# Signs taken from the scaled words, and sixty matmuls on a zero tile in the attention stage

## The chip, the cores and the metric

The kernel runs on one core of a Trainium2 chip. The metric is the device time of one execution in microseconds; the time of a kernel is the median of its runs. The core has five engines that run side by side and wait for each other by semaphores: PE (TensorE, the matmuls; PEld is its loading of weights), DVE (VectorE), ACT (ScalarE), POOL (GpSimd) and SP, which here only issues DMAs. Each engine works through its own instructions in the order in which they were put down.

## The reference

Three stages follow each other; all inputs are float32 in meaning, but the weights arrive as float64 words.

```python
# B, H, S, D = 2, 8, 768, 64;  n_sink = 4, window = 128
scores = scale * q @ k.T
keep = (key < n_sink) | ((0 <= query - key) & (query - key < window))
a = softmax(where(keep, scores, -1e9))
x = (a @ v) as 1536 tokens x 512
# phase 0: 512 -> 2048 -> 512
h = maximum(x @ w_in, 0);  x = (h * h) @ w_out
# phase 1: 512 -> 2048 -> 512
h = x @ w_in2
P = a0 + a1*h + a2*h**2 + a3*h**3
Q = 1 + abs(b0)*abs(h) + abs(b1)*h**2
out = (P / (Q + 1e-6)) @ w_out2
```

## The kernel before, in words

**Attention** goes by 24 steps (batch, block of 256 queries, pair of heads). A step's work is a generator in four pieces (lines 304 to 391): scores of two query blocks by matmul (`s`, L329, or L331 and L332 for batch 1), mask and row maximum on DVE (L340, L341), exponentials on ACT (L348), division (`rs` on DVE, L352 on POOL); then the transposes `pt` and `sx` on PE (L357, L360) and their copies; then the product with the values `xo` (L382 to L386), which ACT and DVE split into a high part `xh` (L389) and a low part `xl` (L390). `att_pieces` (L491) interleaves three steps: the two score pieces of step t, one piece of step t-1, one of step t-2.

**The two dense phases** use float32 in two parts: each product is three matmuls, high by high, low by high and high by low. A unit is one chunk of 128 hidden columns for one group of 512 tokens (256 in the first sub-chunk of phase 0): `gemm1` (L394) makes `h` by 12 matmuls, ACT and DVE apply the function (`sq`, L128 and L130, in phase 0), ACT rounds it to `gh` (L407), POOL takes the rest `gl` (L409); `gemm2` (L415) adds 12 matmuls into four accumulators. The first units run between the last attention steps.

**Weights** come in chunks of 1024 columns (`load_chunk`, L292), each in two halves of 512 columns. One half passes through `narrowed` (L53): a DMA brings the float64 words into `wr` (three buffers); its high words `hi` lie at every second position. ACT scales them by 2^-112 into `wt` (L63, two buffers) and writes their sign into the upper half of a word of a `sign` tile (L65, two tiles in turn). DVE ORs the shifted low words with the sign (L66, result back in `wr`) and merges them into `wt` (L67). Then ACT rounds `wt` to `wh` (L299) and POOL writes the remainder `wl` (L300), after which `wt` is free; `wr` is free after L67. There are seven chunk slots in the attention stage and four more after it; a chunk's slot is loaded anew when the last group of tokens has used it, so loading comes in four bursts after the start.

**The order.** A scheduler of the framework puts the instructions of each engine into an order by a timeline that it estimates; the code's order and the dependences between tiles are what it starts from. Whatever it puts first on an engine must finish before the next one there starts.

Of the kernel before, what the change touches and what calls it, by code (L numbers as in the profile page):

```python
# [8 lines left out]
F32 = mybir.dt.float32  # L9
F32R = mybir.dt.float32r  # L10
F16 = mybir.dt.float16
# [9 lines left out]
P = 128  # L21
# [12 lines left out]
SC = (6, 5, 5)  # L34
WSLOTS = 7
MORE = 4
RATE = 0.5
LN2_64 = 64.0 * math.log(2.0)


def f32(ap):
    return ap.bitcast(F32)
# [10 lines left out]
def narrowed(nc, pool, src, n, signs):  # L53

    raw = pool.tile([P, 512, 2], U32, tag="wr", name=f"wr{n}", bufs=3)
    nc.sync.dma_start(raw.rearrange("p c w -> p (c w)"), src.bitcast(U32))
    lo, hi = raw[:, :, 0], raw[:, :, 1]
    t = pool.tile([P, 512], U32, tag="wt", name=f"wt{n}")
    s = signs[0]
    signs.append(signs.pop(0))  # L60


    nc.scalar.mul(f32(t), f32(hi), 2.0**-112)  # L63

    nc.scalar.mul(s.bitcast(F16).rearrange("p (c w) -> p c w", w=2)[:, :, 1], f32(hi), 2.0**-112)  # L65
    nc.vector.scalar_tensor_tensor(out=lo, in0=lo, scalar=29, in1=s, op0=ALU.logical_shift_right, op1=ALU.bitwise_or)  # L66
    nc.vector.scalar_tensor_tensor(out=t, in0=t, scalar=3, in1=lo, op0=ALU.logical_shift_left, op1=ALU.bitwise_or)  # L67
    return f32(t)
# [3 lines left out]
def body(ctx, tc, qk0, qk1, vb, vs, nw, wp, ab, out):  # L72
# [32 lines left out]
    with ExitStack() as fast:  # L105

        banded(fast, tc, const, qk0, qk1, vb, vs, rawf[:, 0:1], rawf[:, 2:3], wp, abt, scalars, out)
# [68 lines left out]
def banded(ctx, tc, const, qk0, qk1, vb, vs, ns_f, win_f, wp, ab, scalars, out):  # L176
    nc = tc.nc
# [4 lines left out]
    gpool = ctx.enter_context(tc.tile_pool(name="gpool", bufs=2))  # L182
# [4 lines left out]
    ps_a2 = att_ctx.enter_context(tc.tile_pool(name="ps_a2", bufs=2, space=PSUM))  # L187
# [15 lines left out]
    def load_pair(bb, j, hp):  # L203
        n = f"{bb}_{j}_{hp}"
        w = 256 + (K0 if j == 0 else K1)
        src = qk0[bb, hp] if j == 0 else qk1[bb, j - 1, hp]

        if bb == 0:
            r = at.tile([P, 256 + K1], F32, tag="qkr", name=f"qkr{n}", bufs=3)
            nc.sync.dma_start(r[:, :w], src)  # L210
            qk = r, None
        else:
            qk = [], []
            for hd in range(2):

                r = at.tile([P, 256 + K1], F32, tag="qkr", name=f"qkr{n}{hd}", bufs=3)
                for i in range(2):
                    nc.sync.dma_start(r[i * D : i * D + D, :w], src[hd * D : hd * D + D])
                t = at.tile([P, 256 + K1], F32R, tag="qk", name=f"qk{n}{hd}", bufs=3)
                kl = at.tile([P, K1], F32R, tag="kl", name=f"kl{n}{hd}", bufs=3)  # L220
                nc.scalar.copy(t[:, :w], r[:, :w])

                nc.vector.tensor_tensor(out=t[64:128, :256], in0=r[64:128, :256], in1=f32(t[64:128, :256]), op=ALU.subtract)
                nc.gpsimd.tensor_tensor(out=kl[:, : w - 256], in0=r[:, 256:w], in1=f32(t[:, 256:w]), op=ALU.subtract)
                qk[0].append(t)
                qk[1].append(kl)
        nb = 2 if j == 0 else 3
        v = at.tile([P, 3, P], F32, tag="v", name=f"v{n}")
        nc.sync.dma_start(v[:, :nb, :], vb[bb, 2 * j + 2 - nb : 2 * j + 2, :, hp * P : (hp + 1) * P].rearrange("i p d -> p i d"))
        if bb not in vst:  # L230

            r = wraw.tile([P, 512, 2], U32, tag="wr", name=f"vsr{bb}", bufs=3)
            r = f32(r.rearrange("p c w -> p (c w)"))[:, : HP * P].rearrange("p (h c) -> p h c", h=HP)
            nc.sync.dma_start(r, vs[bb])
            vh = at.tile([P, HP, P], F32R, tag="vsh", name=f"vsh{bb}", bufs=2)
            vl = at.tile([P, HP, P], F32R, tag="vsl", name=f"vsl{bb}", bufs=2)
            nc.scalar.copy(vh, r)
            nc.gpsimd.tensor_tensor(out=vl, in0=r, in1=f32(vh), op=ALU.subtract)
            vst[bb] = vh, vl
        loaded[bb, j, hp] = *qk, v  # L240

    load_pair(0, 0, 0)


    ident = ac.tile([P, P], F32, name="ident")
# [46 lines left out]
    def load_chunk(L, pool=wpool):  # L292
        home[L] = pool
        h = pool.tile([P, 1024], F32R, tag="wh", name=f"wh{L}")
        lo = pool.tile([P, 1024], F32R, tag="wl", name=f"wl{L}")
        for i in range(2):
            c = slice(i * 512, (i + 1) * 512)
            t = narrowed(nc, wraw, wp[L][:, c], f"{L}_{i}", signs)
            nc.scalar.copy(h[:, c], t)  # L299
            nc.gpsimd.tensor_tensor(out=lo[:, c], in0=t, in1=f32(h[:, c]), op=ALU.subtract)  # L300
        wh[L], wl[L] = h, lo
# [173 lines left out]
    start = [(g, c0, 256) for g in range(3) for c0 in (0, 256)]  # L475
# [15 lines left out]
    def att_pieces():  # L491
        live = {}
        for t in range(len(todo) + 2):
            for s_ in (t, t - 1, t - 2):
                if s_ < 0 or s_ >= len(todo):
                    continue
                if s_ == t:
                    live[s_] = attention(*todo[s_])
                    if fetch:
                        load_pair(*fetch.pop(0))  # L500
                    for _ in range(2):
                        next(live[s_])
                        yield
                else:
                    next(live[s_])
                    yield
            if t >= 2:
                done[t - 2] = True

    att = att_pieces()  # L510

    def att_until(step):
# [21 lines left out]
    for i2 in range(N):  # L534
        look = 2 if i2 < n0 else 3
        work = []
        while i1 < N and i1 <= i2 + look:
# [3 lines left out]
            if i1 == n0:  # L541
                att_ctx.close()
                tb = ctx.enter_context(tc.tile_pool(name="tb", bufs=3))

                more = ctx.enter_context(tc.tile_pool(name="more", bufs=MORE))
                for _ in range(MORE):
                    load_chunk(nxt, more)
# [9 lines left out]
        for w_ in work:  # L557
            for _ in w_:
                if i2 < n0:

                    owed += RATE
                    while owed >= 1:
# [10 lines left out]
def dense(tc, qk0, qk1, vb, ns_f, win_f, wp, ab, out):  # L573
# [75 lines left out]
    with xT_ctx, ExitStack() as ctx:  # L649
        wk = ctx.enter_context(tc.tile_pool(name="d_f", bufs=2))  # L650
        ps_a = ctx.enter_context(tc.tile_pool(name="d_pa", bufs=4, space=PSUM))
        ps_h = ctx.enter_context(tc.tile_pool(name="d_ph", bufs=2, space=PSUM))
        for ph in range(2):
            X = yT if ph else xT
            for g in range(NT // 512):
                cols = slice(g * 512, (g + 1) * 512)
                acc = [ps_a.tile([P, 512], F32, tag="acc", name="d_acc") for _ in range(4)]
                for f in range(NF):
                    wi = narrowed(nc, wk, wp[ph * NF + f][:, 0:512], f"d{ph}{g}{f}i", signs)
                    wo = narrowed(nc, wk, wp[ph * NF + f][:, 512:1024], f"d{ph}{g}{f}o", signs)  # L660
                    h = ps_h.tile([P, 512], F32, tag="h", name="d_h")
                    for k in range(4):
                        nc.tensor.matmul(h, lhsT=wi[:, k * P : (k + 1) * P], rhs=X[:, k, cols], start=k == 0, stop=k == 3)
                    y = rational(nc, wk, h, ab, con) if ph else squared_relu(nc, wk, h)
                    for m in range(4):
                        blk = slice(m * P, (m + 1) * P)
                        l, r = (y[:, blk], wo) if ph else (wo[:, blk], y)
                        nc.tensor.matmul(acc[m], lhsT=l, rhs=r, start=f == 0, stop=f == NF - 1)
                for m in range(4):
                    if ph == 0:  # L670
                        nc.vector.tensor_copy(yT[:, m, cols], acc[m])
                    else:
                        o = wk.tile([P, 512], F32, tag="o", name="d_out")
                        nc.scalar.mul(o, acc[m], -1.0)
                        t0 = g * 512 + m * P
                        nc.sync.dma_start(out[t0 : t0 + P, :], o)
# [58 lines left out]
```

## Time and profile before

| what | value |
|---|---|
| median of 3 runs | 687.01 us (686.88 to 688.39) |
| the profiled execution, its own time | 685.88 us |
| its span (first to last instruction) | 684.2 us |
| busy: PE, PEld | 648.0 us (95%), 528.2 us (77%) |
| busy: DVE, ACT, POOL | 467.9, 460.1, 401.5 us |
| bytes read from HBM | 50.27 MB |

The profile is one execution. Busy time is a share of the whole span, and the stages differ: attention runs from 0 to about 206 us with the first dense units in it, the first instructions of phase 1 stand at about 410 us. A matmul counts as busy for its whole duration whatever the clock of TensorE is, so a slow matmul looks busier than a fast one.

### The profile page before, as it was taken

The numbers are of one execution on the slowest core, as the hardware profiler recorded it, in microseconds if no ns is written. First come the engines' busy times: TensorE is split into PE (matmuls) and PEld (weight loads), VectorE is DVE, ScalarE is ACT, GpSimd is POOL, SyncE is SP. The second block draws the span as 40 slices with busy tenths as digits, with TensorE's granted clock in tenths as the row PEclk, the third lists the DMA queues.
The fourth block names the chain that finished last, engine by engine and source line by source line (L and its number), as shares of the span: only waits on it lengthen the run. The fifth ranks groups of instructions, "written<-read, shape, count | busy, mean of one in ns | idle before, by whom it ended". The sixth has DMA issues, their size and how long they took to land.

```text
span 684.2 us, 10131 instructions
## 1 busy us (share of the span) xinstructions
PE 648.0 (95%) x3376; PEld 528.2 (77%) x3376; DVE 467.9 (68%) x969; ACT 460.1 (67%) x938; POOL 401.5 (59%) x367
## 2 busy tenths in 40 slices
PE   4799999999999997999999998899998999999995
PEld 2456779999999875888778886688887888888884
DVE  7878855879842897427631279976699777577674
ACT  6767755777654876427542489886899866766761
POOL 4757855788753776327454579654577644544441
PEclk9999999999999999899999999999999999999998
DMA  7546632354200645204500033200030000001011
GB/s 249 186 134 184 204 90 69 103 135 131 67 25 1 210 160 182 65 1 137 171 0 1 0 124 103 82 1 1 1 123 32 0 1 1 0 1 61 3 61 68
DMA packets 25725, 54.16 MB, mean 79 GB/s; under 512 B 2880, under 2 KB 11072, under 8 KB 25664
## 3 DMA queue, kind: packets, MB, share of 16 engines
q1 hardware_dynamic: 25664, 53.43, 24.5%
q8 instruction: 29, 0.48, 0.3%
q14 instruction: 32, 0.26, 0.1%
HBM read 50.27 MB, written 3.15 MB: 78 GB/s over the span
## 4 chain that ended last, share of the span: by engine, by line
PE 63%; DVE 16%; ACT 8%; DMA 7%; issue 3%; POOL 2%; DVEq 0%; POOLq 0%; ACTq 0%
PE h L400 27%; PE acc L441 14%; PE acc L439 13%; DMA wr<-in_wp 6%; DVE wt L67 5%; DVE wr L66 4%; PE xo L382 3%; ACT sign L65 2%; PE pt L357 1%; PE s L329 1%; ACT wh L299 1%; ACT wt L63 1%; PE xo L385 1%; PE s L332 1%; POOL wl L300 1%
## 5 line engine op out<-in xcount | busy, mean ns | idle before, releaser
L409 POOL TENSOR_TENSOR gl<-sq,gh 128x256 fp32r<-128x256 f32 (+1 forms) x66 | 72.0, 1093 | 80.3 <-ACT gh L407 45.8
L164 POOL TENSOR_TENSOR z<-z,u 128x512 f32<-128x512 f32 x48 | 63.6, 1326 | 84.8 <-ACT z L163 81.5
L300 POOL TENSOR_TENSOR wl<-wt,wh 128x512 fp32r<-128x512 f32 x64 | 91.4, 1439 | 19.9 <-ACT wh L299 19.9
L66 DVE SCALAR_TENSOR_TENSOR wr<-wr,sign 128x512 uint32<-128x512 uint32 x64 | 64.2, 1003 | 19.6 <-ACT sign L65 19.5
L409 POOL TENSOR_TENSOR gl<-z,gh 128x512 fp32r<-128x512 f32 x47 | 62.1, 1322 | 24.8 <-ACT gh L407 21.2
L67 DVE SCALAR_TENSOR_TENSOR wt<-wt,wr 128x512 uint32<-128x512 uint32 x64 | 68.4, 1069 | 10.9 <-ACT wt L63 10.3
L130 DVE TENSOR_TENSOR sq<-sq,h 128x256 f32<-128x256 f32 (+1 forms) x66 | 35.5, 538 | 58.9 <-ACT sq L128 58.1
L439 PE MATMUL acc<-gh,wh 128*128 128x256 f32 (+1 forms) x264 | 66.2, 339 | 5.6 <-ACT sq L128 4.1
L65 ACT ACTIVATE sign<-wr 128x512 f16<-128x512 f32 x64 | 50.6, 790 | 24.6 <-DMA wr<-in_wp 24.4
L439 PE MATMUL acc<-gl,wh 128*128 128x256 f32 (+1 forms) x264 | 64.9, 336 | 0.5 <-POOL gl L409 0.5
L439 PE MATMUL acc<-gh,wl 128*128 128x256 f32 (+1 forms) x264 | 64.7, 334 | 0.0
L170 DVE SCALAR_TENSOR_TENSOR z<-z,con,h 128x512 f32<-128x512 f32 x48 | 35.8, 745 | 41.6 <-ACT h L169 40.1
L400 PE MATMUL h<-xh,wh 128*128 128x256 f32 (+1 forms) x264 | 61.6, 347 | 0.5 <-DVE sq L130 0.5
L128 ACT ACTIVATE sq<-h 128x256 f32<-128x256 f32 (+1 forms) x66 | 31.5, 477 | 45.3 <-PE h L400 34.5
L441 PE MATMUL acc<-wh,gh 128*128 128x512 f32 x192 | 60.2, 393 | 1.2 <-ACT gh L407 1.2
L441 PE MATMUL acc<-wl,gh 128*128 128x512 f32 x192 | 59.6, 390 | 0.0
L400 PE MATMUL h<-x2h,wh 128*128 128x512 f32 x192 | 53.9, 398 | 4.6 <-DVE z L172 4.6
L400 PE MATMUL h<-xl,wh 128*128 128x256 f32 (+1 forms) x264 | 58.2, 337 | 0.0
L400 PE MATMUL h<-xh,wl 128*128 128x256 f32 (+1 forms) x264 | 58.2, 338 | 0.0
L441 PE MATMUL acc<-wh,gl 128*128 128x512 f32 x192 | 57.6, 389 | 0.0
L439 PEld LDWEIGHTS acc<-gh,wh 128*128 128x128 f32 x264 | 44.5, 192 | 13.4 <-ACT wh L299 4.8
L352 POOL TENSOR_TENSOR e<-e,rs 128x320 f32<-128x320 f32 x48 | 37.2, 778 | 28.0 <-DVE rs L350 20.4
(104 smaller groups left out, 1591.9 us busy)
## 6 DMA issues: line engine op xcount, KB each, us to landing
wr<-in_wp SPq DMA_DIRECT2D x64, 512.0 KB, 3.7
qkr<-in_qk SPq DMA_DIRECT2D x32, 176.0 KB, 3.1
v<-in_vb SPq DMA_DIRECT2D x16, 192.0 KB, 2.7
out<-accsb SPq DMA_DIRECT2D x12, 256.0 KB, 2.1
qkr<-in_qk SPq DMA_DIRECT2D x8, 352.0 KB, 3.5
qkr<-in_qk SPq DMA_DIRECT2D x16, 136.0 KB, 2.8
qkr<-in_qk SPq DMA_DIRECT2D x4, 272.0 KB, 5.0
v<-in_vb SPq DMA_DIRECT2D x8, 128.0 KB, 3.6
```

The costliest lines, as they stand in the source:

```text
L65: nc.scalar.mul(s.bitcast(F16).rearrange("p (c w) -> p c w", w=2)[:, :, 1], f32(hi), 2.0**-112)
L66: nc.vector.scalar_tensor_tensor(out=lo, in0=lo, scalar=29, in1=s, op0=ALU.logical_shift_right, op1=ALU.bitwise_or)
L67: nc.vector.scalar_tensor_tensor(out=t, in0=t, scalar=3, in1=lo, op0=ALU.logical_shift_left, op1=ALU.bitwise_or)
L130: nc.vector.tensor_tensor(out=r, in0=r, in1=h, op=ALU.mult)
L164: nc.gpsimd.tensor_tensor(out=z, in0=z, in1=u, op=ALU.mult)
L170: nc.vector.scalar_tensor_tensor(out=z, in0=z, scalar=con[:, 2:3], in1=h, op0=ALU.add, op1=ALU.mult)
L300: nc.gpsimd.tensor_tensor(out=lo[:, c], in0=t, in1=f32(h[:, c]), op=ALU.subtract)
L352: nc.gpsimd.tensor_tensor(out=eq, in0=eq, in1=rs[:, c].unsqueeze(2).to_broadcast([P, 2, W]), op=ALU.mult)
L400: nc.tensor.matmul(h[:, :n], lhsT=w_[:, k * P : (k + 1) * P], rhs=x_[:, k, c0 : c0 + n], start=p_ + k == 0, stop=p_ + k == 5)
L409: eng.tensor_tensor(out=gl[:, :n], in0=y, in1=f32(gh[:, :n]), op=ALU.subtract)
L439: nc.tensor.matmul(acc[m][:, :n], lhsT=w_[:, 512 + m * P : 512 + (m + 1) * P], rhs=g_[:, :n], start=st, stop=sp, skip_group_check=True)
L441: nc.tensor.matmul(acc[m], lhsT=g_[:, m * P : (m + 1) * P], rhs=w_[:, 512:1024], start=st, stop=sp)
```

## The change

Two edits. In `narrowed` the signs are written from `wt`, the scaled copy that L63 has just made, in place of the strided high words in `wr`. In `banded`, a tile `idle` of 128x512 zeros is made on POOL right after the first attention load; it takes one of the two `gh` buffers, and an accumulator tile of the first units serves as output. `keep_busy` issues ten matmuls of 128x512 on it, once ahead of the attention and once after the score pieces of each of the steps 0 to 4: sixty in all. Only the first of each ten is held at its place in the program's order. Nobody reads what they write.

```diff
@@ constants
+IDLE = 10
@@ narrowed
     nc.scalar.mul(f32(t), f32(hi), 2.0**-112)
 
-    nc.scalar.mul(s.bitcast(F16).rearrange("p (c w) -> p c w", w=2)[:, :, 1], f32(hi), 2.0**-112)
+    nc.scalar.mul(s.bitcast(F16).rearrange("p (c w) -> p c w", w=2)[:, :, 1], f32(t), 1.0)
@@ banded, after load_pair(0, 0, 0)
+    idle = gpool.tile([P, 512], F32R, tag="gh", name="idle")
+    nc.gpsimd.memset(f32(idle), 0.0)
@@ att_pieces
                     for _ in range(2):
                         next(live[s_])
                         yield
+                    if t <= 4:
+                        keep_busy()
@@ ahead of att = att_pieces()
+    idle_ps = ps_a2.tile([P, 512], F32, tag="acc", name="idle_ps")
+
+    def keep_busy():
+        for i in range(IDLE):
+            ins = nc.tensor.matmul(idle_ps, lhsT=idle[:, 0:P], rhs=idle, start=True, stop=True)
+            if i == 0:
+                tc.keep_in_program_order(ins)
+
+    keep_busy()
     att = att_pieces()
```

Because the scheduler makes the order, both edits move instructions on every engine. Three places matter below. The line numbers of the changed kernel are higher by 1 to 4 here: L64 is the old L63 (`wt`), L66 the old L65 (`sign`), L67 and L68 the old L66 and L67, L129 the old L128, L303 the old L299, L411 the old L407.

First, PE at the start of attention; names end in batch block, pair of heads and tile number. Before:

```order
L329 MATMUL s_0_0_00_167<-qkr_0_0_103 128x160
L329 MATMUL s_0_0_01_169<-qkr_0_0_103 128x160
L329 MATMUL s_0_0_10_178<-qkr_0_0_103 128x288
L329 MATMUL s_0_0_11_180<-qkr_0_0_103 128x288
L329 MATMUL s_0_1_00_259<-qkr_0_1_159 128x160
```

Now:

```order
L521 MATMUL idle_ps<-idle 128x512 x10
L333 MATMUL s_0_0_00_180<-qkr_0_0_103 128x160
L333 MATMUL s_0_0_01_182<-qkr_0_0_103 128x160
L333 MATMUL s_0_0_10_191<-qkr_0_0_103 128x288
L333 MATMUL s_0_0_11_193<-qkr_0_0_103 128x288
L521 MATMUL idle_ps<-idle 128x512 x10
L333 MATMUL s_0_1_00_282<-qkr_0_1_172 128x160
```

Ten matmuls stand ahead of the first scores, and ten between each two steps; the later tens stand just ahead of the transposes of the step before.

Second, DVE after the masks are made. Before:

```order
L341 ISA e_0_0_166,nm_0_0_163<-s_0_0_01_169,add_115 128x160
L341 ISA nm_0_0_163 128x1
L340 COPY_PREDICATED s_0_0_10_178<-own_u,s_0_0_10_178 128x128
L341 ISA e_0_0_166,nm_0_0_163<-s_0_0_10_178,add_116 128x160
L341 ISA nm_0_0_163 128x1
L340 COPY_PREDICATED s_0_0_11_180<-own_u,s_0_0_11_180 128x128
L349 TENSOR_SCALAR rs_0_0_165<-sm_0_0_164 128x2
```

Now:

```order
L345 ISA e_0_0_179,nm_0_0_176<-s_0_0_01_182,add_117 128x160
L345 ISA nm_0_0_176 128x1
L67 SCALAR_TENSOR_TENSOR wr_0_206<-wr_0_206,sign_93 128x512
L344 COPY_PREDICATED s_0_0_10_191<-own_u,s_0_0_10_191 128x128
L344 COPY_PREDICATED s_0_0_11_193<-own_u,s_0_0_11_193 128x128
L353 TENSOR_SCALAR rs_0_0_178<-sm_0_0_177 128x2
L68 SCALAR_TENSOR_TENSOR wt_0_208<-wt_0_208,wr_0_206 128x512
```

The OR of the first half of weights, which came after the maxima of steps 0 and 1 began, now stands ahead of the second half of step 0.

Third, ACT in the first burst of weights after attention, at the last chunk of phase 0 (chunk 15; `wr_0` and `wr_1` are its halves). Before:

```order
L65 ACTIVATE sign_94<-wr_1_3321 128x512
L63 ACTIVATE wt_0_3314<-wr_0_3312 128x512
L65 ACTIVATE sign_93<-wr_0_3332 128x512
L63 ACTIVATE wt_1_3323<-wr_1_3321 128x512
L299 CAST wh_3310<-wt_0_3314 128x512
L128 ACTIVATE sq<-h 128x512
```

Now:

```order
L64 ACTIVATE wt_0_3377<-wr_0_3375 128x512
L66 ACTIVATE sign_93<-wt_0_3377 128x512
L411 CAST gh<-sq 128x512
L64 ACTIVATE wt_1_3386<-wr_1_3384 128x512
L66 ACTIVATE sign_94<-wt_1_3386 128x512
L303 CAST wh_3373<-wt_0_3377 128x512
L129 ACTIVATE sq<-h 128x512
```

Before, a sign of a later half stood ahead of the scaling of an earlier one. Now each sign follows its own scaling, here and in all 64 halves.

## Rows read from the trace of the kernel before

**Rows 1.** The page, the span in 40 slices: busy tenths of PE, granted clock.

```profile
PE   4799999999999997999999998899998999999995
PEclk9999999999999999899999999999999999999998
```

**Rows 2.** Busy time by stretch; columns PE, PEld, DVE, ACT, POOL, clock, DMA.

```profile
0.00:52.00 52.00, 37.88 (x129) 22.02 (x130) 40.21 (x141) 36.18 (x99) 30.55 (x38) 1.00 0.58 191
52.00:85.00 33.00, 30.26 (x192) 22.80 (x190) 30.09 (x92) 25.41 (x72) 25.62 (x27) 0.95 0.63 195
```

**Rows 3.** Timeline of PE: start, us, what.

```profile
45.79 1.33 PE L329 MATMUL s<-qkr 64*128 64x288 f32 x2 [0.53 <-DVE xl L390]
...
52.90 0.72 PE L329 MATMUL s<-qkr 64*128 64x288 f32 x2 [0.28 <-DVE nm L341]
```

**Rows 4.** The chain of waits in order of time, about 25 to 55 us.

```profile
29.68 0.66 PE sx L360 x2
...
50.79 1.31 PE s L329 x4
```

**Rows 5.** The chain of waits in order of time, 255 to 285 us.

```profile
275.00 1.28 PE acc L439 x3
...
280.10 2.73 PE acc L439 x12
```

**Rows 6.** Timelines of DVE, ACT and POOL at the start.

```profile
8.53 0.28 DVE L340 COPY_PREDICATED s<-own_u,s 128x128 f32<-128x128 uint32 x1
11.08 0.69 DVE L66 SCALAR_TENSOR_TENSOR wr<-wr,sign 128x512 uint32<-128x512 uint32 x1 [0.68 <-ACT sign L65]
9.73 0.65 ACT L63 ACTIVATE wt<-wr 128x512 f32<-128x512 f32 x1
10.29 0.76 ACT L65 ACTIVATE sign<-wr 128x512 f16<-128x512 f32 x1
0.80 0.99 POOL L49 MEMSET sign<- 128x512 uint32 x2 [0.29 <-POOLq L725]
```

**Rows 7.** Groups by line, whole run: busy, mean ns, idle before.

```profile
L65 ACT ACTIVATE sign<-wr 128x512 f16<-128x512 f32 x64 | 50.6, 790 | 24.6 <-DMA wr<-in_wp 24.4
L63 ACT ACTIVATE wt<-wr 128x512 f32<-128x512 f32 x64 | 42.3, 663 | 4.4 <-POOL wl L300 4.2
L299 ACT CAST wh<-wt 128x512 fp32r<-128x512 f32 x64 | 38.9, 617 | 11.5 <-DVE wt L67 11.4
L66 DVE SCALAR_TENSOR_TENSOR wr<-wr,sign 128x512 uint32<-128x512 uint32 x64 | 64.2, 1003 | 19.6 <-ACT sign L65 19.5
L67 DVE SCALAR_TENSOR_TENSOR wt<-wt,wr 128x512 uint32<-128x512 uint32 x64 | 68.4, 1069 | 10.9 <-ACT wt L63 10.3
L300 POOL TENSOR_TENSOR wl<-wt,wh 128x512 fp32r<-128x512 f32 x64 | 91.4, 1439 | 19.9 <-ACT wh L299 19.9
```

**Rows 8.** Busy time by stretch, as rows 2, in bursts of weight loading.

```profile
238.00:255.00 17.00, 16.97 (x73) 13.33 (x72) 15.93 (x16) 13.90 (x26) 13.03 (x9) 1.00 0.51 177
255.00:272.00 17.00, 12.93 (x55) 9.87 (x53) 12.07 (x15) 11.72 (x21) 10.80 (x9) 0.96 0.49 163
272.00:289.00 17.00, 16.47 (x62) 13.29 (x63) 9.23 (x14) 8.32 (x15) 6.53 (x6) 0.84 0.29 96
510.00:527.00 17.00, 15.23 (x67) 12.11 (x66) 16.93 (x20) 17.00 (x31) 12.22 (x10) 1.00 0.10 32
```

**Rows 9.** Timelines of ACT and PE in the first burst.

```profile
261.74 0.78 ACT L65 ACTIVATE sign<-wr 128x512 f16<-128x512 f32 x1 [1.64 <-DMA wr<-in_wp]
265.31 0.60 ACT L128 ACTIVATE sq<-h 128x512 f32<-128x512 f32 x1
272.53 0.76 PE L439 MATMUL acc<-gh,wh 128*128 128x512 f32 x1 [4.05 <-ACT sq L128]
```

**Rows 10.** Timelines of DVE and ACT: the last half kept ready, and the next scaling.

```profile
86.39 0.69 DVE L66 SCALAR_TENSOR_TENSOR wr<-wr,sign 128x512 uint32<-128x512 uint32 x1
...
220.14 0.67 ACT L63 ACTIVATE wt<-wr 128x512 f32<-128x512 f32 x1
```

## The prediction, made before the changed kernel ran

> **What bounds the kernel now.** I read the busy tenths first. PE is at nine tenths or more in nearly every slice after the fifth [rows 1], so whatever moves the time does so by bringing PE to that state earlier, or by filling the few holes behind it. Two kinds of hole are left. One is the start: up to 52 us PE counts as busy for 37.9 us and idle for 14.1 [rows 2], and its matmuls are slow ones. A pair of score matmuls takes 1.33 us at 45.79 and 0.72 us at 52.90 [rows 3]; the ratio 0.54 is that of the two levels of TensorE's clock, 1.2 and 2.4 GHz. The clock column reads 1.00 there all the same, so I go by durations: before about 52 us TensorE stands at the lower level. It rose after an unbroken stretch of score, transpose and value matmuls. The other kind is the bursts of weight loading. In the first, PE is idle for 17.0 - 12.93 = 4.07 us in one stretch and 0.53 in the next, where the granted clock also falls to 0.84 [rows 8]. The timelines say why: ACT stands for 1.64 us on a sign whose DMA has not landed, and the ReLU that PE waits for comes behind it; PE then idles for 4.05 us [rows 9] and runs at the lower level afterwards: three matmuls of 512 columns take 1.28 us (0.427 each) at 275 us, twelve take 2.73 us (0.2275 each) at 280 us [rows 5].
>
> **The change, part by part.**
>
> *Clock at the start.* In the chain of waits from 29.68 to 52.1 us there are 17 pieces of PE work, the first and last of them in [rows 4], together 13.8 us. At the upper level they would take 0.54 of it, so 6.3 us less. Zero if the clock does not rise, so the bounds are 0 and -6.3. I take -6.3, because the first tens run without a gap before and around the first scores, a denser stretch than the one that raised it at 52 us.
>
> *The sixty matmuls.* At the upper level 60 x 0.2275 = 13.7 us of PE, at the lower 60 x 0.427 = 25.6 [rows 5]. The first two tens lie beside the loading of q and k, the masks and the first half of weights; the next two where PE stands idle or DVE holds the chain. The last two (after steps 3 and 4, at about 27 and 38 us) stand ahead of transposes that the chain passes through: 2 x 2.3 = 4.6 us, half of it in PE's holes. I take +2.3; the bounds are 0 (all in the 14.1 us of idle) and +13.7.
>
> Making the zero tile costs POOL another 0.5 us, the half of two such [rows 6]; the index tiles behind it feed the masks, whose work on DVE ends just ahead of 8.53 us and waits for the scalars first, which hides it. The borrowed `gh` buffer and accumulator are given back after the last ten, and no unit needs them before step 4 is through.
>
> *DVE's first wait.* The OR of the first half of weights now stands ahead of the rest of step 0. Its sign comes from the DMA and is there at about 11.05 us as before; before, DVE did attention from 8.53 until 11.08 - 0.68 = 10.40 us [rows 6]. That work of 1.9 us moves behind the OR: +1.9. Bounds 0 and +2.5, the whole wait.
>
> *Signs behind their scalings.* A sign waited for the DMA alone; now it also waits for its `wt` buffer, which comes free only when POOL has written `wl` two halves earlier. Per instruction nothing changes: contiguous words to read may bring 790 ns down towards the 617 of L299, and a sign that began 0.09 us before its scaling had ended (10.29 against 9.73 + 0.65 [rows 6]) must wait for the end; I cost that at nothing, as ACT has room. What changes is what can be done ahead. Before, signs and ORs of three halves were finished while the loading stood still: the last at 86.39 us, though the next scaling came at 220.14 [rows 10]. Now these three ORs fall into the burst. At 0.69 us each undisturbed, that is 2.1 us a burst, and the bound above is 3 x (1.003 + 0.790) = 5.4 at mean durations with the three signs in series [rows 7], below 0. It counts where DVE has nothing to spare: in the first burst (15.9 of 17 us busy) and the last (16.9 of 17) [rows 8]. The third burst hands its last three on to the fourth, so it gains as much as it takes. Together +4.2.
>
> *No sign ahead of an earlier scaling.* Against this, ACT no longer meets a sign whose DMA is under way while scalings with landed data stand behind it. ACT stood idle for 24.4 us for such DMAs in the whole run [rows 7]. What PE lost of it in the first burst is 4.07 us of idle time and 0.16 x 17 = 2.7 us of clock [rows 8], 6.8 together. I take three quarters, -5.1; bounds 0 and -6.8 - 0.5. I stay near the upper end because the new order has scaling, sign, scaling, sign and the two roundings in every unit.
>
> **Sum.** -6.3 + 2.3 + 1.9 + 4.2 - 5.1 = -3.0 us. Against the profiled execution, 685.9, that is 682.9. The median shown is 1.1 us above that execution, so I forecast **684.0 us**. A gain at 52 us is kept because PE is then nearly full up to the first burst [rows 1].
>
> **The rivals.**
>
> *The loop over two `wt` buffers becomes the bound (slower).* Before, a `wt` was held for scaling, merge, rounding and `wl`: 0.663 + 1.069 + 0.617 + 1.439 = 3.79 us [rows 7], two halves at a time. Now the sign and the OR stand inside: + 0.790 + 1.003 = 5.58 us for the two halves that a unit has to itself. A unit of 512 tokens is 24 matmuls, 24 x 0.2275 = 5.46 us [rows 5]. So the loop decides as soon as anything at all stands between. If the ReLU and the rounding of `gh`, 0.6 us each, always do, a unit takes 6.7 us, 1.2 more, over ten units of the first burst +12 us instead of the 6.8 lost now; that is +5.2 where I put -5.1, with 4.2 already counted for the ORs and so partly in it: about 8 worse, 692 us. For it: DVE, which holds the OR and the merge, has no room in that stretch [rows 8]. Against it: an undisturbed OR takes 0.69 us and not the mean of 1.0 [rows 6, 7], which gives the loop half a microsecond back.
>
> *The clock does not rise, or falls between the tens (slower).* The stretches between are small score matmuls and transposes, the kind that left it low for 52 us [rows 3]. Then -6.3 becomes 0 and two tens on the chain cost 2 x 4.3, half covered, +4.3: 684.0 + 6.3 + 2.0 = 692 us. The Trainium skill, "TensorE: Matmul & The Clock Gate", Part 4 (PE-mode transpose), says that transposes do not count as busy work for the clock in the way other matmuls do; by that the clock would fall again where transposes follow a ten, and the outcome would be this one. The stretch that raised it before 52 us held transposes too, but mostly other matmuls, so the trace does not decide.
>
> *DVE takes PE's place at the start (no change).* DVE is busy 40.2 of the first 52 us and 30.1 of the next 33 [rows 2]. If what PE no longer delays runs into DVE's queue, -6.3 + 2.3 shrinks to 0: 688 us.
>
> *Everything is covered (faster still).* The tens all lie in PE's idle time, the whole 6.8 us comes back and the ORs find gaps: -6.3 + 1.9 - 6.8 = -11.2, so 676 us.
>
> **How the numbers follow.** My forecast has a chance of 0.40 with a range of its own of 680 to 688. The full gain has 0.15 (676), DVE as the bound 0.15 (688), the `wt` loop 0.20 (692), the low clock 0.10 (692). About 0.2%, 1.4 us, is what a measurement of this kernel can tell from no change. Faster: 0.36 of the forecast's 0.40, 0.15 and a fifth of DVE's case, 0.54. Within: 0.03 and 0.10, 0.13. Slower: 0.33. The range is **674 to 692**: what it leaves out is the upper part of the two slow cases and a little below the full gain.
>
> **What would show it.** Score pairs at 0.7 us and value matmuls as short as after 52 us, from about 10 us on, show the clock; pairs of 1.33 us after a ten show that it failed. Attention is then ahead: the last `xo` comes before 206 us. DVE should wait from about 8.6 to 11 us for the first sign. In 255 to 289 us PE should be idle for under 2 us and the granted clock at 1.00; the last three ORs before it should lie after 217 us, not before 87. If the idle time before scaling (L63) put down to POOL's `wl` grows from 4.2 us [rows 7] beyond some 15, the `wt` loop is the bound. The forecast is wrong if the first units are not earlier than now, or if the first burst holds PE up longer.

## The result, and the profile after

The changed kernel takes **669.5 us** (median of four runs, 666.82 to 671.14) against 686.94 us of the kernel before on the same chip (four runs, 684.94 to 688.39): a ratio of 0.9744 with a 95% interval of 0.9702 to 0.9787. It is faster, as forecast, but by 17.4 us where 3 were forecast, and it lies below the stated range of 674 to 692. The profiled execution took 670.37 us with a span of 668.6 us, 15.6 less than before.

The page of the changed kernel, busy tenths of PE and granted clock in 40 slices:

```profile
PE   7899999999999999999999999999999999999995
PEclk9899999999999999999999999999999999999999
```

Against [rows 1] the start is fuller (7, 8, 9 for 4, 7, 9) and the sevens and eights further right are gone. A ten of zeros counts as busy, though, so the first slices say little of useful work. The stretches of [rows 2, 8] in the changed kernel, columns as there, and one long stretch for all four bursts:

```profile
0.00:52.00 52.00, 43.52 (x190) 29.57 (x190) 37.36 (x141) 35.42 (x98) 30.79 (x39) 0.87 0.58 192
...
238.00:255.00 17.00, 17.00 (x76) 13.83 (x75) 11.16 (x14) 12.09 (x21) 10.24 (x8) 1.00 0.42 141
255.00:272.00 17.00, 15.78 (x68) 12.33 (x67) 14.05 (x19) 13.22 (x22) 10.89 (x8) 1.00 0.43 147
272.00:289.00 17.00, 17.00 (x75) 13.85 (x74) 10.47 (x13) 11.09 (x19) 10.84 (x8) 1.00 0.50 172
```

```profile
200.00:550.00 350.00, 347.70 (x1608) 285.88 (x1607) 232.49 (x317) 248.38 (x419) 209.82 (x157) 1.00 0.20 68
```

The long stretch and the third and fourth burst in the kernel before, same view:

```profile
200.00:550.00 350.00, 338.05 (x1561) 276.46 (x1560) 225.89 (x301) 234.62 (x401) 204.63 (x152) 0.99 0.20 68
408.00:442.00 34.00, 29.98 (x129) 23.50 (x128) 33.96 (x46) 31.53 (x54) 25.75 (x19) 1.00 0.27 93
490.00:535.00 45.00, 43.23 (x188) 34.84 (x186) 40.19 (x52) 42.49 (x72) 33.05 (x24) 1.00 0.18 59
```

PE idled for 350 - 338.05 = 11.95 us there and now idles for 2.30. The hole of the first burst (4.6 us between 255 and 289 us) is down to 1.22 and the clock stays at 1.00; but the third burst had a hole of 4.0 us too, and the fourth one of 1.8. I had looked into the first burst alone.

The time is best divided at a landmark that all kernels share: the first rounding to `wh` after 200 us, where the first burst begins. In the kernel before, and with the three later bursts' first roundings:

```profile
217.87 0.61 ACT L299 CAST wh<-wt 128x512 fp32r<-128x512 f32 x1
...
306.28 0.61 ACT L299 CAST wh<-wt 128x512 fp32r<-128x512 f32 x1
...
391.25 0.61 ACT L299 CAST wh<-wt 128x512 fp32r<-128x512 f32 x1
...
490.88 0.60 ACT L299 CAST wh<-wt 128x512 fp32r<-128x512 f32 x1
```

The same four in the changed kernel:

```profile
215.46 0.61 ACT L303 CAST wh<-wt 128x512 fp32r<-128x512 f32 x1
...
297.66 0.62 ACT L303 CAST wh<-wt 128x512 fp32r<-128x512 f32 x1
...
380.84 0.62 ACT L303 CAST wh<-wt 128x512 fp32r<-128x512 f32 x1
...
477.57 0.60 ACT L303 CAST wh<-wt 128x512 fp32r<-128x512 f32 x1
```

The lead grows from 2.4 us at the first burst to 8.6, 10.4 and 13.3 us at the next ones and 15.6 at the end. So the start gave 2.4 us and what lies behind it 13.2: the first burst 6.2 of it, the three later stretches 1.8, 2.9 and 2.3, together 7.0. The groups by line that answer to [rows 7]:

```profile
L66 ACT ACTIVATE sign<-wt 128x512 f16<-128x512 f32 x64 | 50.4, 789 | 0.9
L64 ACT ACTIVATE wt<-wr 128x512 f32<-128x512 f32 x64 | 42.6, 665 | 10.7 <-POOL wl L304 8.1 <-DMA wr<-in_wp 2.5
L67 DVE SCALAR_TENSOR_TENSOR wr<-wr,sign 128x512 uint32<-128x512 uint32 x64 | 60.5, 945 | 29.5 <-ACT sign L66 29.5
L68 DVE SCALAR_TENSOR_TENSOR wt<-wt,wr 128x512 uint32<-128x512 uint32 x64 | 65.7, 1026 | 3.8
```

ACT stood idle for 24.4 us for weight DMAs ahead of signs; that is gone, with 2.5 us of it turning up ahead of the scalings. The wait for POOL's `wl` grew from 4.2 to 8.1 us, short of the 15 that the prediction set as the mark of the `wt` loop. The ORs, at the same work, wait longer for their signs and take 945 ns for 1003.

The timeline of PE at the start of the changed kernel, tens of zeros and matmuls of attention:

```profile
2.30 4.63 PE L521 MATMUL idle_ps<-idle 128*128 128x512 f32 x10 [2.30 <-POOL idle L246]
7.96 2.55 PE L521 MATMUL idle_ps<-idle 128*128 128x512 f32 x10
...
13.44 1.21 PE L333 MATMUL s<-qkr 64*128 64x288 f32 x4 [2.45 <-DVE nm L345]
14.57 3.88 PE L521 MATMUL idle_ps<-idle 128*128 128x512 f32 x10
...
21.27 2.57 PE L521 MATMUL idle_ps<-idle 128*128 128x512 f32 x10
25.99 0.87 PE L386 MATMUL xo<-pT,v 128*64 128x256 f32 x8 [1.49 <-DVE rs L354]
30.27 4.51 PE L521 MATMUL idle_ps<-idle 128*128 128x512 f32 x10
```

Ten matmuls in 2.55 us are at the upper level, in 3.88 or 4.51 us wholly or mostly at the lower one. The clock rose and fell again twice within 30 us, each time after PE had stood idle (2.45 us ahead of 13.44, 1.49 ahead of 25.99). The prediction had it up throughout. I go by durations here, as the prediction did: the clock column reads 1.00 up to 52 us in the kernel before too, where the durations show the lower level. The fifth ten stands on the chain that ended last:

```profile
30.34 4.44 PE idle_ps L521 x10
```

It is the first ten on that chain; from 4.13 to 25.99 us the chain has the first weight DMA and then work of ACT and DVE, and no piece of PE. At the lower level the fifth ten took some 2 us longer than the 2.55 of a ten at the upper one.

### The profile page after: what moved, and what is told of

Read it like the earlier page. It is cut to its first block, busy times and chain, and to the rows that moved or that the text cites. A ratio compares the mean times of both kernels' runs of the same rounds, so it can differ in the third digit from the quotient of the medians.

```text
span 668.6 us, 10310 instructions
## 1 busy us (share of the span) xinstructions
PE 650.1 (97%) x3436; PEld 533.4 (80%) x3436; DVE 460.0 (69%) x969; ACT 461.4 (69%) x938; POOL 399.4 (60%) x368
## 4 chain that ended last, share of the span: by engine, by line
PE 72%; DVE 11%; ACT 10%; issue 3%; POOL 2%; DMA 1%; SPq 0%; DVEq 0%; ACTq 0%; POOLq 0%
PE h L404 31%; PE acc L445 15%; PE acc L443 15%; DVE wt L68 4%; DVE wr L67 4%; PE xo L386 3%; ACT sign L66 2%; PE s L333 2%; ACT wt L64 2%; PE pt L361 1%; ACT wh L303 1%; POOL wl L304 1%; PE xo L389 1%; ACT gh L411 1%; PE s L336 1%
## 5 line engine op out<-in xcount | busy, mean ns | idle before, releaser
L413 POOL TENSOR_TENSOR gl<-sq,gh 128x256 fp32r<-128x256 f32 (+1 forms) x66 | 68.8, 1043 | 63.3 <-PE acc L443 25.9
L67 DVE SCALAR_TENSOR_TENSOR wr<-wr,sign 128x512 uint32<-128x512 uint32 x64 | 60.5, 945 | 29.5 <-ACT sign L66 29.5
L68 DVE SCALAR_TENSOR_TENSOR wt<-wt,wr 128x512 uint32<-128x512 uint32 x64 | 65.7, 1026 | 3.8
L129 ACT ACTIVATE sq<-h 128x256 f32<-128x256 f32 (+1 forms) x66 | 31.4, 475 | 40.4 <-PE h L404 31.1
L303 ACT CAST wh<-wt 128x512 fp32r<-128x512 f32 x64 | 39.1, 617 | 26.0 <-DVE wt L68 25.5
L404 PE MATMUL h<-xh,wl 128*128 128x256 f32 (+1 forms) x264 | 56.7, 334 | 0.0
L404 PE MATMUL h<-x2l,wh 128*128 128x512 f32 x192 | 53.6, 396 | 0.0
```

What stands on the lines that cost most here:

```text
L404: nc.tensor.matmul(h[:, :n], lhsT=w_[:, k * P : (k + 1) * P], rhs=x_[:, k, c0 : c0 + n], start=p_ + k == 0, stop=p_ + k == 5)
L413: eng.tensor_tensor(out=gl[:, :n], in0=y, in1=f32(gh[:, :n]), op=ALU.subtract)
```

## The experiments

Two theories stood at the beginning. By the first, the gain is the signs': ACT runs its instructions in order, and a sign that waits for nothing but a DMA stands ahead of work that is due. By the second, the zeros bring it through the clock. (In order does not mean that the records of neighbours never touch: the sign at 10.29 us begins 0.09 us before its scaling has ended [rows 6].) Each table row below has the median, its ratio to the kernel before on the same chip with the 95% interval, the start of the first burst and the rest of the profiled span behind it. The last two are of one execution each. Single runs of one kernel spread over 2 to 4.5 us for most, over 6.5 for e2 and 9 for e5 and the kernel before, so differences of 2 or 3 us in these columns decide nothing. A median with its interval weighs more.

| kernel | median us | ratio | first burst at | rest |
|---|---|---|---|---|
| before | 686.94 | - | 217.87 | 466.3 |
| after: new signs, 60 zeros | 669.5 | 0.9744 (0.9702 to 0.9787) | 215.46 | 453.1 |
| e1: new signs, no zeros | 661.4 | 0.9634 (0.9589 to 0.9679) | 204.41 | 454.7 |
| e2: old signs, 60 zeros | 687.39 | 1.0011 (0.9983 to 1.0038) | 219.44 | 469.2 |
| e3: old source, order held, 60 zeros | 673.46 | 0.9795 (0.9751 to 0.9838) | 216.20 | 456.6 |
| e7: old source, order held, no zeros | 666.39 | 0.9696 (0.9673 to 0.9719) | 210.51 | 457.2 |
| e5: new signs in the first seven slots only | 676.4 | 0.9835 (0.9773 to 0.9898) | 206.98 | 468.9 |
| e6: new signs from the eighth slot on only | 670.89 | 0.9764 (0.974 to 0.9787) | 215.72 | 455.0 |
| e4: new signs, 12 zeros | 663.43 | 0.9668 (0.9622 to 0.9715) | 207.05 | 453.3 |
| e8: new signs, 120 zeros | 682.36 | 0.9934 (0.9911 to 0.9958) | 225.99 | 455.1 |
| e9: new signs, the first ten only | 665.33 | 0.9672 (0.9649 to 0.9695) | 208.58 | 455.1 |
| e10: new signs, tens after steps 0 to 2 only | 665.12 | 0.9689 (0.9655 to 0.9722) | 209.57 | 453.7 |
| e11: new signs, tens after steps 3 and 4 only | 664.19 | 0.9653 (0.9635 to 0.9672) | 208.27 | 454.8 |

### One half of the change alone (e1, e2)

e1 is the kernel before with this line changed and nothing else; e2 is the changed kernel with this line as before.

```diff
-    nc.scalar.mul(s.bitcast(F16).rearrange("p (c w) -> p c w", w=2)[:, :, 1], f32(hi), 2.0**-112)
+    nc.scalar.mul(s.bitcast(F16).rearrange("p (c w) -> p c w", w=2)[:, :, 1], f32(t), 1.0)
```

> The kernel before with the signs edit alone, no matmuls on zeros. Theory A (the signs edit fills PE's holes in the bursts, the zeros only help the start): 672 to 676 us; the first burst starts within 1 us of 217.9 (first wh, L299, after 200 us); PE idle under 3 us between 255 and 345 us against 6.1 before; ACT's idle time ahead of scalings and signs put down to weight DMAs falls from 24.4 to under 6 us. Theory B (the clock and the new order of the start bring most of it): above 680 us.

> The changed kernel with the old sign source, sixty matmuls on zeros kept. Theory A: 683 to 686 us, first burst 2 to 3 us earlier than before (about 215.5), PE's holes in the bursts as before (4 to 5 us in 255 to 289, 4 us in 408 to 442). Theory B: 670 to 676 us.

The signs alone give 661.4 us, a larger gain than both edits together: this one line is the fastest version that ran, and it beats both kernels. Both theories missed it. The first had the bursts right (ACT's idle time for DMAs ahead of signs is gone), but expected 672 us or more and the first burst within 1 us of 217.87, where it begins 13.5 us earlier:

```profile
204.41 0.61 ACT L299 CAST wh<-wt 128x512 fp32r<-128x512 f32 x1
```

The zeros alone change nothing that can be measured (687.39 us). The first theory had expected 683 to 686 and an earlier first burst; it begins 1.6 us later, which is within the scatter. On top of the new signs the same sixty cost 11.05 us at the first burst (215.46 against 204.41), and on top of a held order (e3 against e7, below) 5.7. What the zeros cost thus depends on what else holds the start up. That the old signs covered it is my reading of these three numbers, and no run shows it directly. The groups of the two kernels show where the signs' gain in the bursts sits. e1:

```profile
L65 ACT ACTIVATE sign<-wt 128x512 f16<-128x512 f32 x64 | 50.6, 790 | 0.8
```

e2:

```profile
L66 ACT ACTIVATE sign<-wr 128x512 f16<-128x512 f32 x64 | 50.6, 790 | 27.9 <-DMA wr<-in_wp 27.8
```

The wait for DMAs ahead of signs comes and goes with the source of the sign, whatever the zeros do. PE's busy time from 200 to 550 us goes with it, in e1 and then in e2 (columns PE busy, clock, DMA share, GB/s):

```profile
200.00:550.00 350.00, 346.64 (x1556) 1.00 0.21 68
```

```profile
200.00:550.00 350.00, 337.68 (x1551) 0.99 0.21 68
```

### The order or the words (e3, e7)

The new source does two things: the sign reads contiguous words, and it can't run ahead of its own scaling. In e7 the kernel before keeps the old source, and a dependence that costs no semaphore holds each sign behind its scaling; e3 is the same with the sixty zeros.

```diff
-    nc.scalar.mul(f32(t), f32(hi), 2.0**-112)
+    scaled = nc.scalar.mul(f32(t), f32(hi), 2.0**-112)
...
-    nc.scalar.mul(s.bitcast(F16).rearrange(...)[:, :, 1], f32(hi), 2.0**-112)
+    sign = nc.scalar.mul(s.bitcast(F16).rearrange(...)[:, :, 1], f32(hi), 2.0**-112)
+    if tc is not None:
+        tc.add_manual_dep(
+            sign.ins, scaled.ins.name,
+            ...
+            reason="sign behind its scaling")
```

> The changed kernel, but the sign is written from the strided high words as before, and only held behind its own scaling in ACT's order. If it is the order that fills the holes: 667 to 674 us, and no wait of ACT for a weight DMA with another half's scaling behind it. If the contiguous source or the wait on the data does it: 680 us or more.

> The kernel before, the sign still written from the strided high words, only held behind its scaling in ACT's order; no zeros. If the order is what the signs edit gives: 660 to 666 us, first burst at 204 to 208. If the contiguous source counts too: 667 us or more.

e3 came out as the order was expected to (673.46 us). e7 fell between its two cases: 666.39 us, and a first burst at 210.51 where 204 to 208 was expected. By the medians the order alone gives 20.9 us against e1's 25.3, so it is the larger part of what the signs edit does. With the order alone the rest of the span is 456.6 and 457.2 us, against 466.3 before and 454.7 with the new source: 9.1 of the 11.6 us that e1 gains in the bursts are the order's. At the start e7 reaches the first burst 7.4 us earlier than before, of e1's 13.5. The remainder, 2.5 and 6.1 us in these executions, came with the new source; as e7's was the slowest of its four, 3.1 us above the median, part of it is scatter, and the intervals of the two ratios just touch (0.9673 and 0.9679). The remainder can't be the reading: the group of e7 shows 785 ns for a sign from strided words, where e1's shows 790 from contiguous ones.

```profile
L65 ACT ACTIVATE sign<-wr 128x512 f16<-128x512 f32 x64 | 50.2, 785 | 0.0
L63 ACT ACTIVATE wt<-wr 128x512 f32<-128x512 f32 x64 | 43.0, 672 | 10.1 <-POOL wl L305 9.8
```

The rest of the order differs between the two forms as well, and I did not take that remainder further apart.

### Where the signs' gain lies (e5, e6)

The new source goes to the chunks of the seven slots of the attention stage only (e5), or to the later ones only (e6); neither has zeros.

```diff
-    nc.scalar.mul(s.bitcast(F16).rearrange(...)[:, :, 1], f32(hi), 2.0**-112)
+    if scaled:
+        nc.scalar.mul(s.bitcast(F16).rearrange(...)[:, :, 1], f32(t), 1.0)
+    else:
+        nc.scalar.mul(s.bitcast(F16).rearrange(...)[:, :, 1], f32(hi), 2.0**-112)
...
-            t = narrowed(nc, wraw, wp[L][:, c], f"{L}_{i}", signs)
+            t = narrowed(nc, wraw, wp[L][:, c], f"{L}_{i}", signs, L < 7)   # e6: L >= 7
```

> The kernel before with the new sign source for the chunks 0 to 6 alone (loaded during attention), the old one for the rest, no zeros. Theory A2 (signs and ORs done ahead held up attention at the start, and the same at the bursts): the start gains what it gained with all signs new, first burst at 204 to 208 us instead of 217.9; the bursts keep their holes; total 672 to 677 us. Rival C (the start is won by a chance of the whole order): first burst later than 212 us.

> The opposite: new sign source for chunks 7 to 31 alone, no zeros. Theory A2: first burst at 216 to 219 us as before, but holes in the bursts mostly gone (PE idle under 4 us between 255 and 535 us after the shift, 11 before); total 673 to 678 us. Rival C: the gain does not divide, total below 668 or above 682.

The two gains are separate and nearly add up: e5 brings the first burst forward by 10.9 us and leaves the rest at 468.9, e6 shortens the rest by 11.3 us and brings the start forward by 2.2; e1 has 13.5 and 11.6. The medians say the same, 10.9 and 16.4 us against e1's 25.3. e5 came out as theory A2 has it; e6's 670.89 us lies 2 us below its range, with 3.81 us of PE idle from 200 to 550 us. The landmark of e5:

```profile
206.98 0.61 ACT L302 CAST wh<-wt 128x512 fp32r<-128x512 f32 x1
```

So about half of what the signs are worth lies in the attention stage, where the prediction saw none.

What differs there is in the timelines. DVE of the kernel before: the third and the fifth OR.

```profile
15.42 1.76 DVE L66 SCALAR_TENSOR_TENSOR wr<-wr,sign 128x512 uint32<-128x512 uint32 x1
19.36 0.87 DVE L67 SCALAR_TENSOR_TENSOR wt<-wt,wr 128x512 uint32<-128x512 uint32 x1
...
22.89 1.76 DVE L66 SCALAR_TENSOR_TENSOR wr<-wr,sign 128x512 uint32<-128x512 uint32 x1
...
28.32 0.68 DVE L67 SCALAR_TENSOR_TENSOR wt<-wt,wr 128x512 uint32<-128x512 uint32 x1
```

ACT of the kernel before, where attention step 0 is through with its product:

```profile
25.04 0.36 ACT L389 CAST xh<-xo 128x256 fp32r<-128x256 f32 x1
```

ACT of e1, the same instruction:

```profile
20.92 0.37 ACT L389 CAST xh<-xo 128x256 fp32r<-128x256 f32 x1
```

Before, the third OR was done 2.2 us and the fifth 3.7 us ahead of the merge that needs it. Up to the `xh` of step 0 DVE had done five ORs and four merges (9.4 us in all), in e1 three and two (4.1 us), and ACT six signs against three. The `xh` of step 0 came 4.1 us later. That this work ahead is what delayed it is argued from these timelines; that the early signs delay attention is shown by e5. The delay is complete early on: the first `gh` of the dense units starts at 62.18 us in the kernel before and at 49.00 in e1, 13.2 us earlier, nearly the whole 13.5 of the start.

How much of the start's 13.5 us behind these first 4.1 is order, and how much an earlier clock, stays open. In e1 the clock rose without any zeros, as its timeline of PE shows:

```profile
18.61 1.55 PE L382 MATMUL xo<-pT,v 128*64 128x256 f32 x8 [0.41 <-DVE nm L341]
27.08 1.00 PE L382 MATMUL xo<-pT,v 128*64 128x256 f32 x8
30.55 0.72 PE L329 MATMUL s<-qkr 64*128 64x288 f32 x2 [0.19 <-DVE rs L350]
```

The score pair takes 0.72 us at 30.55, where the kernel before still takes 1.33 at 45.79 [rows 3]. The step that came 4.1 us earlier lies before that rise.

### How much a zero costs (e4, e8)

`IDLE` is set to 2 (twelve zeros) and to 20 (a hundred and twenty) in the changed kernel.

```diff
-IDLE = 10
+IDLE = 2    # e8: IDLE = 20
```

> The changed kernel with two matmuls on zeros in each of the six places in place of ten. If the clock raised by the tens gives the 2.4 us by which the first burst is earlier: first burst back at about 217 us, score pairs 1.3 us up to 45 us and more, total 671 to 674 us. If the order at the start gives it: as the changed kernel, 668 to 671 us, first burst at about 215.5 us.

> The changed kernel with twenty matmuls on zeros in each of the six places. Theory D (zeros cost PE time on the way to the first units and push weights ahead of attention on DVE, and their clock gives little back): first burst 10 us or more later than with ten (225 or later), total 678 us or more. Rival (the clock is worth its matmuls, ten are only too few to hold it): 664 to 670 us.

Both cases of e4 missed: with 663.43 us it is faster than either, so the first burst at 207.05 us belongs to neither. e8 came out as theory D has it. With 0, 12, 60 and 120 zeros the first burst begins at 204.4, 207.1, 215.5 and 226.0 us, and the rest behind it is the same within 2 us. From 12 to 60 that is 0.175 us a zero, from 60 to 120 again 0.175: three quarters of the 0.2275 us that one takes on PE [rows 5] reach the first burst. In e8 the clock was up for most of the start, as its windows and its timeline of PE show:

```profile
0.00:52.00 52.00, 45.58 (x201) 33.51 (x202) 37.63 (x127) 35.68 (x90) 30.39 (x36) 0.97 0.63 204
```

```profile
16.95 4.86 PE L521 MATMUL idle_ps<-idle 128*128 128x512 f32 x20
...
34.80 0.87 PE L386 MATMUL xo<-pT,v 128*64 128x256 f32 x8
```

Twenty zeros in 4.86 us are all at the upper level, and so are the values at 0.87 us; four of the six twenties ran so, the first took 7.12 us and the fourth 6.32. Of all kernels with the new signs in every chunk this is the one with the fullest clock and the latest first burst. The full clock bought the start nothing that covers its price.

### Which tens cost it (e9, e10, e11)

Ten zeros ahead of attention and none later (e9); those after steps 0 to 2 (e10); those after steps 3 and 4 (e11).

```diff
-                    if t <= 4:
+                    if t <= 2:          # e11: if 3 <= t <= 4:   e9: no tens after steps
                         keep_busy()
...
-    keep_busy()                         # kept in e9
     att = att_pieces()
```

> The changed kernel with the first ten matmuls on zeros alone, those ahead of attention. They lie where PE waits for q and k, but with them the order again has the first OR ahead of step 0's second half on DVE, as in the changed kernel; with the signs alone it has not. Theory F (that place in DVE's order costs what was forecast, about 2 us): first burst at 206 to 207 us against 204.4 with no zeros, total 662 to 665 us. Rival G (the tens cost by their PE time alone): first burst at 204 to 205 us, total 660 to 663.

> Thirty zeros, after steps 0, 1 and 2, none ahead of attention and none after 3 and 4. Six tens together put the first burst off by 11 us. If each costs the same: +5.5 us, first burst at 210, total 667. If the early ones are covered, as forecast: under +2 us, total 661 to 664. If the early ones are the dear ones: +7 us and more, total 668 or more.

> Twenty zeros, after steps 3 and 4 alone. If each ten costs the same: +3.7 us, first burst at 208, total 665. The forecast's 2.3 us: 663 to 664, first burst at 206.7. If the clock they hold gives back more than they cost: first burst before 204 us, total under 661.

Against e1's 204.41 the first ten costs 4.2 us, the three in the middle 5.2 and the last two 3.9; together 13.2 where all sixty cost 11.05. e9 lies beyond both of its cases; e10 and e11 came out as equal prices for every ten would have it. So no ten looks free. These are single executions; by the medians the three cost 3.9, 3.7 and 2.8 us over e1, with intervals of the ratios that overlap e1's, so a price for each ten is likely but its size is not settled. The first ten costs most for its length in the landmarks; DVE of e9, of the changed kernel and of e1 shows what differs:

```profile
11.12 0.69 DVE L67 SCALAR_TENSOR_TENSOR wr<-wr,sign 128x512 uint32<-128x512 uint32 x1 [2.44 <-ACT sign L66]
```

```profile
11.29 0.69 DVE L67 SCALAR_TENSOR_TENSOR wr<-wr,sign 128x512 uint32<-128x512 uint32 x1 [3.13 <-ACT sign L66]
```

```profile
12.17 0.70 DVE L66 SCALAR_TENSOR_TENSOR wr<-wr,sign 128x512 uint32<-128x512 uint32 x1 [0.15 <-ACT sign L65]
```

With the ten in front, the order has the first OR ahead of the second half of step 0; in e1, e10 and e11, which lack that ten, it stands behind. DVE waits for 2.44 us there in e9 and for 3.13 us in the changed kernel; in e1 it waits for 0.15. Step 0's `xh` comes at 28.28 in e9 and at 28.53 in the changed kernel, 7.4 and 7.6 us behind e1's; the later steps win some of it back.

The middle tens show in e10's timeline of PE:

```profile
19.44 1.15 PE L333 MATMUL s<-qkr 64*128 64x288 f32 x4 [2.75 <-ACT pa L369]
20.52 3.80 PE L521 MATMUL idle_ps<-idle 128*128 128x512 f32 x10
...
24.91 0.87 PE L386 MATMUL xo<-pT,v 128*64 128x256 f32 x8
```

PE is idle for 2.75 us until the scores can start; the ten behind them then runs for 3.8 us, and the first values come only after it, at 24.91 us, against 18.61 in e1.

## Why the prediction was wrong

The sign of the result was right, the size was not. Counted by the landmark, the start came out near its forecast (-2.1 forecast: -6.3 + 2.3 + 1.9; -2.4 measured), but by luck, since each of its terms was off and a large one was missing. Behind the landmark -0.9 was forecast (+4.2 - 5.1) and -13.2 measured. That is where the forecast broke.

- **"Signs behind their scalings … Together +4.2"** is the first half of the step that failed. It took what the kernel before did ahead of need as a gain that the change would lose. In the bursts the loss cost nothing: the first OR of the first burst now comes at 219.26 us, inside it as foreseen, and PE is idle for 0 us from 238 to 255 us and through the fourth burst, which now begins at 477.57, the two places where +4.2 should have appeared:

```profile
477.57:527.00 49.43, 49.43 (x215) 40.21 (x215) 44.42 (x62) 48.25 (x83) 35.45 (x28) 1.00 0.16 54
```

- **"No sign ahead of an earlier scaling"** (-5.1) is the second half. The mechanism was right; the term was sized for one burst. That burst gave 6.2 us, close to the 6.8 that the prediction read there before it took three quarters; the three later stretches gave 7.0, for which the sum had no term. PE's idle time between 200 and 550 us fell from 11.95 to 2.30 us, and with the clock of the first burst that makes most of the 13.2 us. The group of [rows 7] that named 24.4 us of idle ACT was for the whole run; only [rows 8, 9] of the first burst were asked where it hurt.
- **The missing term.** At the start the work done ahead was itself a cost: new signs in the first seven slots alone bring the first burst forward by 10.9 us (e5), with an earlier clock perhaps in that. The prediction had no term for this, and asked only what the new order delays, never what the old one did.
- **The sixty matmuls** (+2.3) cost about 11 us together with DVE's first wait (+1.9), 4.2 forecast. The middle tens were put at nothing, as lying in PE's idle time or where DVE holds the chain; e10 measures 5.2 us for them. An idle stretch of PE at the start was not free for a filler here: the engine waits there for another one, and in e10 the ten that stands next in the order runs on when the wait is over.
- **DVE's first wait** had the right place. It was costed at the 1.9 us of work that moves behind the OR; e9 shows 4.2 us at the first burst for the ten and the wait together.
- **The clock** (-6.3) was not had as forecast: it rose with the first ten and fell twice before 30 us, and where it stays up for most of the time (e8) the start is no earlier. The reading that it is not the bound there rests on the chains: up to 25.99 us in the changed kernel, and up to 27.11 in e8, no piece of PE's work is on them, only DVE's and ACT's behind the first DMA. No run changed the clock alone, so its own worth stays open. The rival that named DVE as taking PE's place said this, for the clock's term alone.
- **The rivals.** The `wt` loop did not decide (8.1 us of waiting for `wl`; a kernel with a third `wt` buffer was not tried). The low clock was half true: it fell between the tens, and cost some 2 us at the fifth one, which took 4.51 us on the chain. In the changed kernel PE had stood idle before it fell, and whether transposes had a part in it, as the Trainium skill has it ("TensorE: Matmul & The Clock Gate", Part 4), no run here tells. "Everything is covered" came nearest with 676 us, but its reason was wrong for the zeros.
- **The signs that it named.** The first unit's `gh` comes at 58.70 us against 62.18, the last `xo` starts at 203.9 us, before 206; DVE waits for the first sign until 11.29 us; PE is idle for 1.22 us between 255 and 289 with the clock at 1.00; the first OR of the burst lies after 217. Of these signs only that of the clock at the start failed. They tell that the order did what was foreseen, and none of them could tell how much it was worth.
- **Sum by the measured parts**, against the landmark: signs at the start -13.5, zeros +11.05, bursts -11.6 (e1) to -13.2 (changed kernel). That is -14 to -15.6; the profiled spans differ by 15.6. The sum has to come out, as its parts are differences at the same landmark.

## What to carry to other kernels

Work done ahead of need was not free on the in-order engines of this kernel: look for instructions that wait only for a DMA and stand in front of work that is due, and tie them to the step that uses them. Judge fillers for the clock by the time of the work that waits, not by the granted clock: here they cost three quarters of their own length, even where the engine looked idle. And when a cause is found in one stage, ask every other stage for it before sizing it.

## What the runs showed of the hardware that I had not expected

ACT takes 789 ns to write a sign from contiguous words and 785 to 790 ns from strided ones; reading at every second position costs it nothing here. A plain rounding of the same size takes 617 and the scaling, which reads strided words, 663 [rows 7], so most of the surplus lies in something else. The strided 16-bit write is what the two signs share; no run tests it by itself. And TensorE's clock rose without any filler at about 27 us in e1 and fell again, as two short windows of it show (PE busy, clock, DMA share, GB/s):

```profile
36.00:40.00 4.00, 3.44 (x16) 0.70 0.54 178
40.00:44.00 4.00, 4.00 (x16) 0.50 0.51 180
```

The kernel that did this is still the fastest of all that ran.
